# GpSimd operations that wait for VectorE, other places for results, and new times for the list schedule, in a fused attention and expert kernel

## The chip, the cores and the metric

The kernel runs on one core of one Trainium2 chip. A core has five engines with a queue each: TensorE (PE in the profile; its weight loads are listed apart as PEld), VectorE (DVE), ScalarE (ACT), GpSimd (POOL) and SyncE (SP), which here only issues DMAs. The metric is the device time of one execution in microseconds (us); lower is better. Before the change it is 932.47 us, the median of 3 runs (932.33 to 932.93).

## The reference

Attention with pooled keys and values (groups of 8 averaged), then a two-layer network with an unusual activation:

```python
def _attn_ref(q, k, v):                      # B, H, S, D = 8, 8, 576, 64
    k_p = k.reshape(B, H, S // 8, 8, D).mean(axis=3)
    v_p = v.reshape(B, H, S // 8, 8, D).mean(axis=3)
    scores = np.matmul(q, k_p.transpose(0, 1, 3, 2)) / np.sqrt(D)
    scores = scores - np.max(scores, axis=-1, keepdims=True)
    attn = np.exp(scores)
    attn = attn / (np.sum(attn, axis=-1, keepdims=True) + 1e-09)
    return np.matmul(attn, v_p).astype(np.float32)

def _moe_ref(x, w_in, w_out):                # x: 4608 x 512, w_in: 512 x 2048, w_out: 2048 x 512
    h = x @ w_in
    sp = np.maximum(h, 0.0) + np.log1p(np.exp(-np.abs(h)))
    g = h * erf(sp)
    return (g @ w_out).astype(np.float32)
```

## The kernel before, in words

**Tiles and stages.** The 4608 tokens are cut into nine chunks (`ck`) of 512; `w_in` and `w_out` into sixteen pieces of 128 rows of the hidden layer (`ft`). A step is one piece for one chunk, so there are 9 x 16 = 144 steps, two of which make a pair (`pair`). [...] ScalarE or another engine makes the high part by a cast, VectorE or GpSimd the low part by a subtraction: `ql` (L562) for the queries, `gl` (L822) for the activations, L401 for the weights.

**Attention** of a chunk (`job`, `softmax_tile`) runs while the chunk before it is in the network. Keys and values are loaded into `raw` and summed by GpSimd (L504, L506, L508); scores come from L572, L574 and L596; VectorE finds the maximum and subtracts it (L583, L585), ScalarE takes the exponentials, VectorE the sums and reciprocals (L630, L632, L634), GpSimd scales the last columns (L640, `ends`) and VectorE the whole (L644); TensorE transposes (L651, L658) and multiplies with the values (L688).

**The network.** In chunks 0 and 1 the first product is a plain matmul (L787). From chunk 2 (`FROM`) on it is made of seven half-size products (`products`, L733), whose weights are sums of pieces of `w_in`. The function `sums` makes these once, in chunk 1, and writes them to DRAM; from then on the place of `w_in` is free for others: `wi6` to `wi15` are a ring of ten slots into which SP loads the sums again for every pair (four loads a pair), `wi5` holds the accumulator `u` (four rows, one for each pair in turn), `wi0` to `wi4` hold the attention's result, a temporary and the hidden values `hs`. VectorE adds the products together (L751). The activation is Softplus (L805), Erf (L812), a product on VectorE (L815), a cast (L817) and the low part (L822). The second product is L836. After the sixteenth piece of a chunk `store` copies its four results (128 x 512 each) from PSUM into one of the two buffers `f`, on ScalarE (L848) or VectorE (L849), and a DMA takes each to `out`.

**The order.** All five queues are written out by one list scheduler, `Program.order`. Every operation has an engine (or a choice of them), an estimated cost in ns, and a due time `prio` in steps. The scheduler always takes the operation with the smallest sum of its earliest start and `SLACK` (30 ns) a step of due time; operations whose due time is more than `WINDOW` steps beyond the newest one on TensorE aren't looked at. An operation may go to another engine if it ends there at most `BIAS` ns after the end on its own. [...] In the first 57 us, dummy matmuls (`filler`, L884) fill TensorE's gaps.

Of the kernel before, what the change touches and what calls it, by code (L numbers as in the profile page):

```python
# [20 lines left out]
POOL = 8  # L21
# [4 lines left out]
P = 128  # L26
# [9 lines left out]
NB = 2  # L36


WINDOW = 14
SHIFT = 3  # L40
B1 = 2
T0, T0_STEP = -10.5, 0.5
VAL_R = 2.5
KEYS, KEYS_R, KEYS_S = -4.5, 0.4, -1.0
VALS, VALS_R, VALS_S = -1.0, 0.4, -1.2
Q_DUE = 5.2
W_IN, W_OUT = 1.0, 0.0
LEAD = 4
G2 = 5.0
ON_DVE = 2  # L50
CAP_H, CAP_O, CAP_ATT, CAP_CV, CAP_ATT0 = 2, 4, 4, 2, 6
ON_ACT = ((1, 1), (1, 1), (1, 1), (1, 1))
# [2 lines left out]
LENT_Q = ("wi15", "wo12")  # L55
LENT_KV = ("wo8", "wo9", "wo10", "wo11", "wi9", "wi10", "wi11", "wi12", "wi13", "wi14")
WIDE_FROM = 2
SLACK, BIAS = 30, 2000
FILL, MARGIN = 57000.0, 300
DGE = 2000  # L60
TURN = 0.0
# [4 lines left out]
HALF = TC // 2  # L66
PART = {"A11": (0, 0), "A12": (0, 1), "S1": (1, 0), "S3": (1, 1), "S2": (2, 0), "S4": (2, 1), "A22": (3, 0)}
PARTS = 4
RING = tuple(f"wi{i}" for i in range(6, NJ))
XF, TD, UU, HS = ("wi0", "wi1"), "wi2", "wi5", ("wi3", "wi4")  # L70
SUMS, SUMS_R = 2.0, 0.3
X_DUE = 3.0
RING_LEAD = 8.0
C_ID = 0
C_MA = 128
C_MB = 130
# [54 lines left out]
class Op:  # L131
    def __init__(self, eng, cost, prio, fn):
        self.eng, self.cost, self.prio, self.fn = eng, cost, prio, fn
        self.bufs, self.next, self.wait, self.ready = [], [], 0, 0.0
        self.set = None


class Program:
# [49 lines left out]
    def order(self):  # L188
        free = {e: 0.0 for e in self.DELAY}
        free["SP"] = 2400.0  # L190
        slots = {t: [0.0] * n for t, n in self.capacity.items()}
        avail = {e: [] for e in free}
        for i, o in enumerate(self.ops):
            o.key = (o.prio, i)
            if not o.wait:
                for e in o.choice:
                    avail[e].append(o)
        progress, out, loaded, port = 0.0, [], "sigmoid", 0.0
        spare = heapq.heappop(slots["banks"]) if self.filler else None
        for _ in self.ops:  # L200
            best = None
            for e, ops in avail.items():
                pick, ready = None, []
                for o in ops:
                    if o.prio > progress + self.window or any(b.left for b in o.after):
                        continue
                    start = max(o.ready + (DGE if e == "SP" else 0), free[e])
                    switch = SWITCH if o.set and o.set != loaded else 0
                    start += switch
                    if e == "POOL" or o.port and e == "DVE":  # L210
                        start = max(start, port)
                    need = {}
                    for b in o.bufs:
                        if not b.held:
                            for t in b.limits:
                                need[t] = need.get(t, 0) + 1
                    ok = True
                    for t, k in need.items():
                        if len(slots[t]) < k:
                            ok = False  # L220
                            break
                        start = max(start, heapq.nsmallest(k, slots[t])[-1] + (DGE if e == "SP" else 0))
                    if ok and e != o.eng:
                        ok = start + o.choice[e][0] <= max(o.ready, free[o.eng]) + o.cost + BIAS
                    if ok:
                        ready.append((start, o.key, o, start - switch * (1 - TURN) + SLACK * o.prio))
                if ready:
                    pick = min(ready, key=lambda r: (r[3], r[1]))[:3]
                if pick and (best is None or pick[:2] < best[:2]):
                    best = pick + (e,)  # L230
            if best is None:
                raise RuntimeError(("no operation can go on", progress, {e: [(o.prio, [b.args[3] for b in o.bufs if not b.held]) for o in ops][:8] for e, ops in avail.items()}, {k: len(v) for k, v in slots.items()}))
            start, _, o, e = best
            for a in o.choice:
                avail[a].remove(o)
            o.eng, (o.cost, o.fn) = e, o.choice[e]
            loaded = o.set or loaded
            if spare is not None and o.eng == "PE":
                if start > FILL:
                    heapq.heappush(slots["banks"], start)  # L240
                    spare = None
                else:
                    idle = start - max(free["PE"], 3000.0) - MARGIN - (1800 if not free["PE"] else 0)
                    out.extend([self.filler] * int(idle / 107))
            end = free[o.eng] = start + o.cost
            if o.eng == "POOL" or o.port and o.eng == "DVE":
                port = end
            if o.eng == "PE":
                progress = max(progress, o.prio)
            for b in o.bufs:  # L250
                if not b.held:
                    b.held = True
                    for t in b.limits:
                        heapq.heappop(slots[t])
                b.left -= 1
                b.end = max(getattr(b, "end", 0.0), end)
                if not b.left:
                    for t in b.limits:
                        heapq.heappush(slots[t], b.end + 150)
            for d, flow in o.next:  # L260
                if d.eng != o.eng:
                    t = end + self.DELAY[o.eng]
                else:
                    t = end + (self.SAME[o.eng] if flow else 0)
                d.ready = max(d.ready, t)
                d.wait -= 1
                if not d.wait:
                    for a in d.choice:
                        avail[a].append(d)
            out.append(o)  # L270
        self.length = max(free.values())
        return out
# [10 lines left out]
def moe_attention(ctx: ExitStack, tc: tile.TileContext, cst, qa, kl, vl, wi, wo, out):  # L283
# [204 lines left out]
    def job(ck, b, tiles, off, times, first, fresh):  # L488
# [60 lines left out]
        def softmax_tile(at, qo, T, r):  # L549
# [9 lines left out]
            copy(ck < 2, 4 * T, r - 0.6, lambda: qh.ap[:, :, :T], lambda: raw.ap[:, :, :T], [raw], [qh])  # L559

            def low(e):
                e.tensor_sub(ql.ap[:, :, :T], raw.ap[:, :, :T], f32(qh.ap[:, :, :T]))  # L562

            op("POOL", gps(4 * T), r - 0.5, lambda: low(nc.gpsimd), [raw, qh], [ql],
               alt=("DVE", dve(4 * T), lambda: low(nc.vector)) if first else None, port=True)
# [71 lines left out]
            def ends():  # L637
                sv = s.ap[:T].rearrange("t (p x) k -> t p x k", x=2)[:, :, 1, P - SP:]
                zv = z.ap[:T].rearrange("t (p x) -> t p x", x=2)[:, :, 1]
                nc.gpsimd.tensor_mul(bb.ap[:T], sv, zv.unsqueeze(2).broadcast_to([T, NP, 16]))  # L640

            op("POOL", gps(64), r + 1.2, ends, [s, z], [bb])

# [35 lines left out]
        for p in range(NP):  # L679
# [8 lines left out]
                    nc.tensor.matmul(d, w, e, start=(i == 0), stop=(i == 3), skip_group_check=True)  # L688

            r = due + p * 0.4  # L690
            op("PE", 3 * (n / 2.4 + 13) + n / 2.4 + 13, r, values, [eth, etl, etb, VA, VB], [pv])
            if ck >= FROM:
                x = xk[p // 2]
                after(op("ACT", act(n, True), r + 0.4, lambda p=p, pv=pv, x=x: nc.scalar.copy(
# [9 lines left out]

    po = {}

    common = late(UU, [4, HALF])

    def products(n, unit, hs):

# [28 lines left out]
        def multiply(prio, b, *what):  # L739
            def run():  # L740
                for j, (side, name, t, first) in enumerate(what):
                    product(side(b), name, t, first)

            reads = [parts[PART[name][0]] for _, name, _, _ in what] + [ts[ck, t] for _, _, t, _ in what]
            op("PE", 6 * 119 * len(what), prio, run, reads, [b])

        u, j = common, n // 2 % 4
        lo, hi = slice(0, HALF), slice(HALF, TC)

        def add(prio, dst, x, b, side, reads, writes):  # L750
# [18 lines left out]
    def pair(n):  # L769
# [44 lines left out]
        for k in range(2):  # L814
            op("DVE", dve(TC), n + 1.9, lambda k=k: nc.vector.tensor_mul(  # L815
                g(k), y.ap[:, half(k)], hh[k].ap), [(y, k), hh[k]], [gs[k]], port=kept)
            op("ACT", act(TC), n + 2.0, lambda k=k: nc.scalar.copy(gh[k].ap, g(k)), [gs[k]], [gh[k]], port=True,  # L817
               alt=("DVE", 0.52 * TC + 150, lambda k=k: nc.vector.tensor_copy(gh[k].ap, g(k)))
               if COPY_DVE > 1 and not kept else None)

            def low(e, k=k):
                e.tensor_sub(gl[k].ap, g(k), f32(gh[k].ap))  # L822

            both(True, dve(TC), gps(TC), n + 2.0, low, [gs[k], gh[k]], [gl[k]])

        for u, (ck, ft) in enumerate(units):
            if ft == 0:
                po[ck] = [bank("o") for _ in range(TC // P)]
            for t0 in range(0, TC // P, 1 if split else 2):
                ts = range(t0, t0 + (1 if split else 2))  # L830

                def gemm2(u=u, ft=ft, ts=ts, o=po[ck]):
# [4 lines left out]
                                             start=(ft == 0 and q == 0), stop=(ft == NJ - 1 and q == 2))  # L837

                prio = n + u + G2 + 0.1 * t0
                op("PE", 3 * 229 * len(ts), prio, gemm2, [gh[u], gl[u], w_out[ft]],  # L840
                   [po[ck][t] for t in ts])
                if ft == NJ - 1:
                    for t in ts:
                        store(ck, t, po[ck][t], prio + 0.1, ck == NC - 1)

    def store(ck, t, o, prio, last):
        ot, r0 = buf("gh" if last and t % 2 else "f", [DM]), TC * ck + P * t
        op("ACT", act(512, True), prio, lambda: nc.scalar.copy(ot.ap, o.ap), [o], [ot],  # L848
           alt=("DVE", dve(512), lambda: nc.vector.tensor_copy(ot.ap, o.ap)))  # L849
        save = lambda e: e.dma_start(out[r0:r0 + P, :], ot.ap)  # L850
        if last and t % 2:
            op("ACT", 100, prio, lambda: save(nc.scalar), [ot], [])
        else:
            op("SP", 800, prio, lambda: save(nc.sync), [ot], [])


    steps = [(ck, ft) for ck in range(NC) for ft in range(NJ)]
# [26 lines left out]
    pr.filler = Op("PE", 107, 0, lambda: nc.tensor.matmul(  # L884
        idle.ap[:, :256], cb[:, :P], cb[:, :256], start=True, stop=True))
    for o in pr.order():
        o.fn()


# [35 lines left out]
```

## Time and profile before

| | |
|---|---|
| median of 3 runs | 932.47 us |
| the profiled execution | 932.53 us |
| its span, from the first instruction to the last | 930.8 us |
| granted TensorE clock, mean | 0.999 |

The page gives each engine's busy time and its share of the span; the windows view gives the same for stretches of time; the view of waits adds up who stood idle until whom; the chain is followed back from the last instruction to whatever released each step. A matmul's end is modelled, and consecutive matmuls overlap in the records, so TensorE's busy time hides a part of each short stall.

```profile
PE   8999999999999999999999999999999999999998
DVE  6998784899977787777667776767667856664342
POOL 2589886445543244427351144344553322120000
DMA  9991234245396446755575356643776355546511
```

Each digit is the busy share of a fortieth of the span, in tenths. The first three slices, about 70 us, are the head: the weights are loaded, and the first chunk's attention has to be through before the network starts.

### The profile page before, as it was taken

The page shows a single profiled execution, that of the slowest core. Times are in us where ns is not written, and L with a number is a line of the kernel's source. Part 1 is how long each engine was busy: PE and PEld are TensorE (multiplying, and loading weights), DVE is VectorE, ACT ScalarE, POOL GpSimd, SP SyncE. Part 2 cuts the span into 40 slices and gives each one's busy share as a digit, 9 for nine tenths or more (in the row PEclk, how much of TensorE's full clock was granted, in tenths as well). Part 3 has the DMA queues.
Part 4 walks back from the last instruction along what each step waited for, and adds up shares of the span by engine and source line. Part 5 has one row for each costly group of instructions (what it writes and reads, how often), then busy time and mean ns, then how long its engine had stood idle before and what let it go on. Part 6 is the DMA issues. An engine that isn't in the chain of part 4 may idle for free.

```text
span 930.8 us, 16115 instructions
## 1 busy us (share of the span) xinstructions
PE 910.0 (98%) x5655; PEld 802.2 (86%) x5655; DVE 665.4 (71%) x1361; ACT 682.1 (73%) x1209; POOL 382.1 (41%) x475
## 2 busy tenths in 40 slices
PE   8999999999999999999999999999999999999998
PEld 7778878788888889899989888989998899888996
DVE  6998784899977787777667776767667856664342
ACT  4889995987677686876777767766886777665664
POOL 2589886445543244427351144344553322120000
PEclk9999999999999999999999999999999999999999
DMA  9991234245396446755575356643776355546511
GB/s 317 402 396 66 94 113 139 114 182 196 112 345 214 155 166 219 255 195 193 185 246 184 129 196 238 216 170 140 244 237 204 124 202 173 164 160 211 181 53 46
DMA packets 68257, 176.24 MB, mean 189 GB/s; under 512 B 11216, under 2 KB 13392, under 8 KB 68176
## 3 DMA queue, kind: packets, MB, share of 16 engines
q1 hardware_dynamic: 67888, 174.69, 54.4%
q8 instruction: 45, 0.74, 0.3%
q10 hardware_dynamic: 288, 0.52, 0.1%
q14 instruction: 36, 0.29, 0.1%
HBM read 151.06 MB, written 24.12 MB: 188 GB/s over the span
## 4 chain that ended last, share of the span: by engine, by line
PE 65%; DVE 8%; ACT 8%; DMA 5%; POOL 3%; issue 2%; SPq 0%; POOLq 0%; DVEq 0%; ACTq 0%
PE banks L836 32%; PE banks L733 24%; DMA out<-f 4%; PE banks L787 3%; PE banks L688 3%; ACT L805 2%; ACT y L805 1%; PE banks L572 1%; ACT y L812 1%; ACT L812 1%; PE banks L651 1%; DMA raw<-vl 1%; DVE wi L815 1%; DVE hs L815 1%; POOL gl L822 1%
## 5 line engine op out<-in xcount | busy, mean ns | idle before, releaser
L836 PE MATMUL banks<-wo,gh 128*128 128x512 f32 x1152 | 363.8, 397 | 1.7 <-DVE hs L751 0.8
L733 PE MATMUL banks<-t,wi 128*128 128x256 f32 x2352 | 314.3, 284 | 3.9 <-DVE wi L751 1.6
L733 PEld LDWEIGHTS banks<-t,wi 128*128 128x128 f32 x2352 | 300.8, 191 | 18.2 <-DVE wi L751 3.6
L836 PEld LDWEIGHTS banks<-wo,gh 128*128 128x128 f32 x1152 | 203.2, 189 | 36.0 <-DVE hs L751 1.0
L836 PE MATMUL banks<-wo,gl 128*128 128x512 f32 x576 | 225.2, 391 | 0.1
L836 PEld LDWEIGHTS banks<-wo,gl 128*128 128x128 f32 x576 | 108.2, 188 | 24.9 <-DVE gl L822 0.9
L805 ACT ACT_TABLE_LOAD x72 | 92.4, 1283 | 28.9 <-DVE wi L751 15.3
L751 DVE TENSOR_TENSOR wi<-wi,banks 128x256 f32<-128x256 f32 x168 | 67.1, 414 | 44.7 <-ACT wi L754 22.3
L787 PE MATMUL banks<-t,wi 128*128 128x512 f32 x384 | 92.6, 393 | 1.6 <-DVE f L849 1.1
L787 PEld LDWEIGHTS banks<-t,wi 128*128 128x128 f32 x384 | 70.9, 188 | 17.7 <-DVE f L849 1.3
L504 POOL TENSOR_TENSOR raw<-raw 128x256 f32<-128x256 f32 (+1 forms) x60 | 51.5, 861 | 82.8 <-DMA raw<-vl 52.7
L562 POOL TENSOR_TENSOR ql<-raw,qh 128x512 fp32r<-128x512 f32 (+1 forms) x36 | 46.6, 1295 | 74.2 <-ACT qh L324 68.1
L812 ACT ACTIVATE y<-y 128x1024 f32<-128x1024 f32 (+1 forms) x73 | 76.2, 1046 | 0.7
L812 ACT ACT_TABLE_LOAD x59 | 75.7, 1283 | 1.0
L817 ACT CAST gh<-hs 128x512 fp32r<-128x512 f32 x72 | 44.2, 618 | 30.4 <-DVE hs L815 17.3
L815 DVE TENSOR_TENSOR hs<-y,hs 128x512 f32<-128x512 f32 x72 | 54.0, 790 | 6.4 <-ACT y L812 6.4
L822 DVE TENSOR_TENSOR gl<-hs,gh 128x512 fp32r<-128x512 f32 x54 | 39.8, 744 | 18.6 <-ACT gh L817 18.1
L815 DVE TENSOR_TENSOR wi<-y,wi 128x512 f32<-128x512 f32 x56 | 40.5, 761 | 13.8 <-ACT y L812 13.7
L817 ACT CAST gh<-wi 128x512 fp32r<-128x512 f32 x56 | 34.2, 618 | 21.9 <-PE banks L836 10.5
L751 DVE TENSOR_TENSOR hs<-wi,banks 128x256 f32<-128x256 f32 x84 | 32.8, 415 | 23.7 <-PE banks L733 22.9
L668 POOL TENSOR_SCALAR etb<-etb 32x256 fp32r<-32x256 f32 (+1 forms) x38 | 16.0, 421 | 72.8 <-ACT etb L663 54.7
L822 POOL TENSOR_TENSOR gl<-wi,gh 128x512 fp32r<-128x512 f32 x19 | 25.8, 1359 | 43.0 <-ACT gh L817 23.9
(159 smaller groups left out, 1554.8 us busy)
## 6 DMA issues: line engine op xcount, KB each, us to landing
wi<-w SPq DMA_DIRECT2D x168, 512.0 KB, 4.6
wi<-w SPq DMA_DIRECT2D x56, 256.0 KB, 2.7
raw<-vl SPq DMA_DIRECT2D x36, 256.0 KB, 4.4
out<-f SPq DMA_DIRECT2D x34, 256.0 KB, 4.1
wi<-wi SPq DMA_DIRECT2D x16, 512.0 KB, 7.6
wo<-wo SPq DMA_DIRECT2D x16, 512.0 KB, 8.8
w<-t SPq DMA_DIRECT2D x16, 512.0 KB, 3.1
raw<-kl SPq DMA_DIRECT2D x26, 288.0 KB, 3.2
```

Source lines behind the costliest of these rows:

```text
L504: op("POOL", gps(4 * size), prio, lambda: nc.gpsimd.tensor_add(t.ap[:, 0:4], t.ap[:, 0:4], t.ap[:, 4:8]), [t], [t])
L562: e.tensor_sub(ql.ap[:, :, :T], raw.ap[:, :, :T], f32(qh.ap[:, :, :T]))
L688: nc.tensor.matmul(d, w, e, start=(i == 0), stop=(i == 3), skip_group_check=True)
L733: nc.tensor.matmul(dst(), weight(name, w, p), x[:, xl, p, :], start=(first and p == 0 and q == 0), stop=(p == 1 and q == 2), skip_group_ch ...
L751: return op("DVE", dve(HALF), prio, lambda: nc.vector.tensor_add(dst(), x(), b.ap[:, side]), reads + [b], writes)
L787: nc.tensor.matmul(ph.ap, w_in[ft].ap[:, w, P * p:P * p + P], xs[p].ap[:, x], start=(p == 0 and q == 0), stop=(p == NP - 1 and q == 2))
L805: nc.scalar.activation(y.ap[:, half(k)], hh[k].ap, AF.Softplus)
L812: op("ACT", act(w), n + 1.9, lambda sl=sl: nc.scalar.activation(y.ap[:, sl], y.ap[:, sl], AF.Erf), own, own, funcs="sigmoid")
L815: op("DVE", dve(TC), n + 1.9, lambda k=k: nc.vector.tensor_mul(g(k), y.ap[:, half(k)], hh[k].ap), [(y, k), hh[k]], [gs[k]], port=kept)
L817: op("ACT", act(TC), n + 2.0, lambda k=k: nc.scalar.copy(gh[k].ap, g(k)), [gs[k]], [gh[k]], port=True, alt=("DVE", 0.52 * TC + 150, lambda ...
L822: e.tensor_sub(gl[k].ap, g(k), f32(gh[k].ap))
L836: nc.tensor.matmul(o[t].ap, g.ap[:, gs], w_out[ft].ap[:, w], start=(ft == 0 and q == 0), stop=(ft == NJ - 1 and q == 2))
```

## The change

It has three parts.

1. The scheduler remembers the last marked VectorE operation it has placed (`shared`). A GpSimd operation that could have started before that operation's end plus 600 ns (`APART`) is given a dependency on it, so that on the chip GpSimd waits for it.
2. From chunk 1 to the last but one, three of a chunk's four results no longer go through `f`: two go to `wi6`, which leaves the ring (now nine slots), and one to the upper half of `wi5`, of which `u` keeps two rows in place of four.
3. The due times, the window, `BIAS`, and some cost estimates of TensorE's operations have new values.

```diff
-WINDOW = 14
+WINDOW = 8
-T0, T0_STEP = -10.5, 0.5
-VAL_R = 2.5
-KEYS, KEYS_R, KEYS_S = -4.5, 0.4, -1.0
-VALS, VALS_R, VALS_S = -1.0, 0.4, -1.2
+T0, T0_STEP = -10.5, 0.45
+VAL_R = 2.1
+KEYS, KEYS_R, KEYS_S = -5.5, 0.4, -0.5
+VALS, VALS_R, VALS_S = -1.0, 0.4, -1.1
-W_IN, W_OUT = 1.0, 0.0
-LEAD = 4
-G2 = 5.0
+W_IN, W_OUT = 1.4, 0.1
+LEAD = 4.25
+G2 = 5.2
-SLACK, BIAS = 30, 2000
+SLACK, BIAS = 30, 1150
-RING = tuple(f"wi{i}" for i in range(6, NJ))
-XF, TD, UU, HS = ("wi0", "wi1"), "wi2", "wi5", ("wi3", "wi4")
-SUMS, SUMS_R = 2.0, 0.3
-X_DUE = 3.0
-RING_LEAD = 8.0
+RING = tuple(f"wi{i}" for i in range(7, NJ))
+XF, TD, UU, HS, OUT = ("wi0", "wi1"), "wi2", "wi5", ("wi3", "wi4"), "wi6"
+SUMS, SUMS_R = 4.3, 0.3
+X_DUE = 2.6
+RING_LEAD = 6.25
+APART = 600
...
+            was = free[o.eng]
             end = free[o.eng] = start + o.cost
+            o.end = end
+            if o.eng == "POOL" and shared and max(o.ready, was) < shared.end + APART:
+                o.behind = shared
             if o.eng == "POOL" or o.port and o.eng == "DVE":
                 port = end
+                if o.eng == "DVE":
+                    shared = o
...
-            op("PE", 3 * (n / 2.4 + 13) + n / 2.4 + 13, r, values, [eth, etl, etb, VA, VB], [pv])
+            op("PE", 4 * max(n / 2.4 + 13, 112), r, values, [eth, etl, etb, VA, VB], [pv])
...
-    common = late(UU, [4, HALF])
+    common, outs = late(UU, [4, HALF]), late(OUT, [2, DM])
...
-            op("PE", 6 * 119 * len(what), prio, run, reads, [b])
-
-        u, j = common, n // 2 % 4
+            op("PE", 6 * 120 * len(what), prio, run, reads, [b])
+
+        u, j = common, n // 2 % 2
...
-                op("PE", 3 * 229 * len(ts), prio, gemm2, [gh[u], gl[u], w_out[ft]],
+                op("PE", 3 * 231 * len(ts), prio, gemm2, [gh[u], gl[u], w_out[ft]],
...
-        ot, r0 = buf("gh" if last and t % 2 else "f", [DM]), TC * ck + P * t
-        op("ACT", act(512, True), prio, lambda: nc.scalar.copy(ot.ap, o.ap), [o], [ot],
-           alt=("DVE", dve(512), lambda: nc.vector.tensor_copy(ot.ap, o.ap)))
-        save = lambda e: e.dma_start(out[r0:r0 + P, :], ot.ap)
+        r0 = TC * ck + P * t
+        if ck >= FROM - 1 and not last and t < 3:
+            kept = common if t == 2 else outs
+            key, piece = (kept, ("out", t)), w_in[5 if t == 2 else 6]
+            at = lambda: kept.ap[:, 2:4].rearrange("p a f -> p (a f)") if t == 2 else kept.ap[:, t]
+        else:
+            kept = key = buf("gh" if last and t % 2 else "f", [DM])
+            piece, at = None, lambda: kept.ap
+        after(op("ACT", act(512, True), prio, lambda: nc.scalar.copy(at(), o.ap), [o], [key],
+                 alt=("DVE", dve(512), lambda: nc.vector.tensor_copy(at(), o.ap))), *[piece] * bool(piece))
+        save = lambda e: e.dma_start(out[r0:r0 + P, :], at())
...
     for o in pr.order():
-        o.fn()
+        o.inst = o.fn()
+        if o.behind:
+            tc.add_manual_dep(getattr(o.inst, "ins", o.inst), getattr(o.behind.inst, "ins", o.behind.inst).name,
+                              mybir.DependencyInfo(mybir.DependencyClass.Sync, mybir.DependencyReason.SCHED_ONLY),
+                              reason="port")
```

More of the change, by code (lines that the diff above doesn't have):

```diff
@@ L134, in __init__ @@
         self.bufs, self.next, self.wait, self.ready = [], [], 0, 0.0
-        self.set = None
+        self.set, self.behind = None, None
 class Program:
@@ L197, in order @@
                     avail[e].append(o)
-        progress, out, loaded, port = 0.0, [], "sigmoid", 0.0
+        progress, out, loaded, port, shared = 0.0, [], "sigmoid", 0.0, None
         spare = heapq.heappop(slots["banks"]) if self.filler else None
@@ L561, in low @@
             def low(e):
-                e.tensor_sub(ql.ap[:, :, :T], raw.ap[:, :, :T], f32(qh.ap[:, :, :T]))
+                return e.tensor_sub(ql.ap[:, :, :T], raw.ap[:, :, :T], f32(qh.ap[:, :, :T]))
             op("POOL", gps(4 * T), r - 0.5, lambda: low(nc.gpsimd), [raw, qh], [ql],
@@ L639, in ends @@
                 zv = z.ap[:T].rearrange("t (p x) -> t p x", x=2)[:, :, 1]
-                nc.gpsimd.tensor_mul(bb.ap[:T], sv, zv.unsqueeze(2).broadcast_to([T, NP, 16]))
+                return nc.gpsimd.tensor_mul(bb.ap[:T], sv, zv.unsqueeze(2).broadcast_to([T, NP, 16]))
             op("POOL", gps(64), r + 1.2, ends, [s, z], [bb])
@@ L821, in low @@
             def low(e, k=k):
-                e.tensor_sub(gl[k].ap, g(k), f32(gh[k].ap))
+                return e.tensor_sub(gl[k].ap, g(k), f32(gh[k].ap))
             both(True, dve(TC), gps(TC), n + 2.0, low, [gs[k], gh[k]], [gl[k]])
@@ L846, in store @@
     def store(ck, t, o, prio, last):
-        ot, r0 = buf("gh" if last and t % 2 else "f", [DM]), TC * ck + P * t
-        op("ACT", act(512, True), prio, lambda: nc.scalar.copy(ot.ap, o.ap), [o], [ot],
-           alt=("DVE", dve(512), lambda: nc.vector.tensor_copy(ot.ap, o.ap)))
-        save = lambda e: e.dma_start(out[r0:r0 + P, :], ot.ap)
+        r0 = TC * ck + P * t
[9 more added lines that the diff above has]
+        save = lambda e: e.dma_start(out[r0:r0 + P, :], at())
         if last and t % 2:
-            op("ACT", 100, prio, lambda: save(nc.scalar), [ot], [])
+            op("ACT", 100, prio, lambda: save(nc.scalar), [key], [])
         else:
-            op("SP", 800, prio, lambda: save(nc.sync), [ot], [])
+            op("SP", 800, prio, lambda: save(nc.sync), [key], [])
     steps = [(ck, ft) for ck in range(NC) for ft in range(NJ)]
```

## The prediction

> **What bounds the kernel now.** I read the page's spans first, then the windows view by stage, then the longest waits, the chain that ended last, and the timeline at single stalls.
>
> ```profile
> span 930.8 us, 16115 instructions
> PE 910.0 (98%) x5655; PEld 802.2 (86%) x5655; DVE 665.4 (71%) x1361; ACT 682.1 (73%) x1209; POOL 382.1 (41%) x475
> ```
>
> ```profile
> 0.00:60.00 60.00, 54.66 (x421) 46.74 (x422) 50.02 (x117) 40.47 (x127) 31.43 (x47) 1.00 0.99 369
> 60.00:180.00 120.00, 118.20 (x574) 96.28 (x573) 90.89 (x175) 102.64 (x175) 94.40 (x111) 1.00 0.35 123
> 180.00:926.00 746.00, 736.84 (x4663) 659.22 (x4662) 524.53 (x1071) 538.16 (x908) 256.29 (x318) 1.00 0.55 186
> ```
>
> The columns of the windows view are the stretch, its length, and PE, PEld, DVE, ACT and POOL busy; then clock, DMA share, GB/s. TensorE is the bound: from 60 to 926 us it stands idle for only 1.80 + 9.16 us. The change removes no kernel matmul, so it can only save those gaps and part of the head. Busy time hides some of each gap:
>
> ```profile
> L836 PE MATMUL banks<-wo,gh 128*128 128x512 f32 x1152 | 363.8, 397 | 1.7 <-DVE hs L751 0.8
> 911.32 15.00 PE banks L836 x66
> L884 PE MATMUL banks<-cst 128*128 128x256 bf16 x227 | 29.3, 289 | 2.6 <-DMA cst<-cst 2.6
> ```
>
> One 512-wide matmul shows 397 ns but follows the last every 15.00/66 = 227 ns, so a stall costs about 0.17 us more than the idle it shows. The third row is filler: 29.3 of the head's 54.66 busy us are dummy matmuls, so real work there is 25.4 us of 60.
>
> **The change, part by part.**
>
> *1. Places for results.* Today every result is copied into one of two `f` buffers (L848 on ScalarE, L849 on VectorE) and leaves by a DMA; the third copy of a chunk waits for the first DMA to land, and all behind it in that in-order queue waits too.
>
> ```profile
> ACT f L848 <- DMA out<-f: 6.8, 3, 2.8
> DVE f L849 <- DMA out<-f: 6.5, 3, 3.5
> ```
>
> ```profile
> 263.59 6.29 DMA out<-f
> 366.31 5.10 DMA out<-f
> 462.34 6.63 DMA out<-f
> 562.67 7.13 DMA out<-f
> 849.99 5.57 DMA out<-f
> ```
>
> The chain view's columns are start, length and what. Five chunk ends have an output transfer on the chain that ended last, which a kernel with PE at 98% should not have. I put a window round each (264 to 276, 366 to 374, 462 to 473, 562 to 573, 850 to 859); their sum:
>
> ```profile
> sum 51.00, PE 47.30 PEld 42.41 DVE 30.34 ACT 32.51 POOL 15.96; mean PE 9.46 PEld 8.48 DVE 6.07 ACT 6.50 POOL 3.19
> ```
>
> 51.00 - 47.30 = 3.70 us idle, in about seven stalls: with 7 x 0.17 it is 4.9 us. After the change three of four results of chunks 1 to 7 have a place of their own, reused only a chunk later, and the fourth finds `f` free. I take -4.5, leaving 0.4 because other work shares these windows; bounds 0 and -4.9. What is late next there is the ordinary work in the queues. The price: `wi6` leaves the ring (nine slots, not ten) and `u` has two rows, not four.
>
> ```profile
> wi<-w SPq DMA_DIRECT2D x168, 512.0 KB, 4.6
> ```
>
> A ring load lands in 4.6 us. Four loads serve a pair of steps, and a step lasts about (926 - 60)/144 = 6.0 us; nine slots are 2.25 pairs, 27 us, of which a pair in use takes 12. A lead of 6.25 steps is 38 us, so the ring, not the lead, decides, and some 15 us cover 4.6. I price it at 0; with the cover gone a late load would cost up to 4.6 us. The two rows of `u` turn over every 24 us: 0.
>
> *2. GpSimd behind VectorE.* That the two engines hold each other up is in the durations:
>
> ```profile
> L815 DVE TENSOR_TENSOR hs<-y,hs x72: 677/685/1789, 166.2 to 909.2; 128x512 f32<-128x512 f32 x72
> L815 DVE TENSOR_TENSOR wi<-y,wi x56: 673/685/1796, 276.5 to 917.4; 128x512 f32<-128x512 f32 x56
> L751 DVE TENSOR_TENSOR wi<-wi,banks x168: 360/417/423, 250.1 to 911.7; 128x256 f32<-128x256 f32 x168
> ```
>
> Minimum, median, maximum: L815, whose two inputs are in SBUF, goes from 685 to 1796 ns; L751, with one input in PSUM, never passes 423. One case where TensorE pays:
>
> ```profile
> 389.18 0.29 POOL L640 TENSOR_TENSOR bb<-s,z 128x64 f32<-128x64 f32 x1 [2.22 <-ACT vah L528]
> 389.27 0.75 DVE L822 TENSOR_TENSOR gl<-hs,gh 128x512 fp32r<-128x512 f32 x1
> 389.43 1.74 POOL L562 TENSOR_TENSOR ql<-raw,qh 128x512 fp32r<-128x512 f32 x1
> 389.94 1.84 DVE L644 TENSOR_TENSOR s<-s,z 128x576 f32<-128x576 f32 x1
> 391.93 0.41 PE L651 MATMUL banks<-cst,s 128*128 128x128 f32 x2 [0.83 <-DVE s L644]
> ```
>
> L644 stands at 1.84 us, ends about when L562 does plus its own 0.7, and PE waits 0.83. Eight such places (128 to 132, 320 to 325, 361 to 365, 387 to 393, 538 to 545, 621 to 627, 702 to 706, 809 to 814) sum to
>
> ```profile
> sum 41.00, PE 38.56 PEld 32.66 DVE 36.36 ACT 24.41 POOL 26.37; mean PE 4.82 PEld 4.08 DVE 4.54 ACT 3.05 POOL 3.30
> ```
>
> 2.44 us idle; with some nine stalls of 0.17, 3.9 us. A wait cures only operations that the list marks for the port. L585 isn't marked:
>
> ```profile
> L585 DVE TENSOR_TENSOR s<-s,m 128x576 f32<-128x576 f32 x25 | 23.6, 944 | 0.7
> L644 DVE TENSOR_TENSOR s<-s,z 128x576 f32<-128x576 f32 x28 | 25.7, 918 | 3.2 <-POOL bb L640 3.1
> L815 DVE TENSOR_TENSOR hs<-y,hs 128x512 f32<-128x512 f32 x72 | 54.0, 790 | 6.4 <-ACT y L812 6.4
> L815 DVE TENSOR_TENSOR wi<-y,wi 128x512 f32<-128x512 f32 x56 | 40.5, 761 | 13.8 <-ACT y L812 13.7
> ```
>
> ```profile
> L644 DVE TENSOR_TENSOR s<-s,z x35: 741/752/1851, 23.3 to 799.7; 128x576 f32<-128x576 f32 x28, 64x576 f32<-64x576 f32 x7
> ```
>
> Against a median of 752 ns for this size, L585 loses 25 x 0.19 = 4.8 us and L644 28 x 0.17 = 4.6; L815 loses 72 x 0.105 + 56 x 0.076 = 11.8. So 23% of this loss is uncovered, and a wait is given only where the list has the two within 600 ns; I allow as much again for places where the chip has drifted further. That leaves 60%: **-2.4**, bounds 0 and -3.9, if the waits cost nothing.
>
> What they cost: behind the waiting instruction stand all later GpSimd ones, and for those wait TensorE (`ql`, `gl`), VectorE (L644 behind L640) and SP's loads into `raw`. [...] L640 follows L634, which ended at 389.00 (388.81 + 0.19), by 0.18 us:
>
> ```profile
> 388.81 0.19 DVE L634 RECIPROCAL z<-z 128x8 f32<-128x8 f32 x1
> ```
>
> After 180 us GpSimd is busy 256 of 746 us: taken as 0 there. For 60 to 180 see the rivals.
>
> [...]
>
> *3. BIAS 2000 to 1150.* Work that VectorE and GpSimd can both do goes to the slower one less readily.
>
> ```profile
> L822 POOL TENSOR_TENSOR gl<-wi,gh 128x512 fp32r<-128x512 f32 x19 | 25.8, 1359 | 43.0 <-ACT gh L817 23.9 <-issue 8.3 <-PE banks L688 6.9
> L822 DVE TENSOR_TENSOR gl<-wi,gh 128x512 fp32r<-128x512 f32 x37 | 27.4, 747 | 18.7 <-ACT gh L817 18.5
> ```
>
> Each move is 0.61 us shorter for its reader and 0.75 more on VectorE, which is at 71%. I take 0; bounds -1 and +1.
>
> *4. Due times, window, PE costs.* A unit of due time weighs 30 ns in the list's choice (SLACK), so shifts of 0.05 to 2.3 units turn only near-ties. The window (14 to 8 units, 84 to 48 us) matters in the head, where no step has moved the list's progress yet: it holds back early weight splitting. I take 0 here; bounds -4 (below) and +2.5.
>
> **Sum:** 932.5 (the profiled execution; span 930.8 and 1.7 around it; the median of the runs, 932.47, is the same) - 4.5 - 2.4 = **925.6**.
>
> **Rivals.**
>
> *A. The head shortens too.* VectorE is busy 50.02 of the first 60 us, and some of it is weight splitting in front of the first attention tiles:
>
> ```profile
> L385 DVE SCALAR_TENSOR_TENSOR banks<-banks,hs 128x512 uint32<-128x512 uint32 x6 | 4.1, 689 | 0.0
> L395 DVE SCALAR_TENSOR_TENSOR f<-wi,banks 128x512 uint32<-128x512 uint32 x4 | 2.7, 682 | 0.0
> ```
>
> That is 6.8 us; if 4 of it moves behind the first chunk's attention, PE, whose real work is 25.4 of 60, starts 4 us sooner: 921.5. Against: DMA is 0.99 busy there.
>
> *B. The waits do nothing.* If the chip's order is further from the list than 600 ns, VectorE is blocked as before: 925.6 + 2.4 = 928.0. [...]
>
> *C. New stalls.* The list is made anew. The 9.16 us of idle after 180 hold the 3.70 and about 2.4 of parts 1 and 2; some 3.1 are accidents of order. If the new order has three times as many: 925.6 + 6.2 = 931.8, the same as before.
>
> *D. GpSimd becomes the bound between 60 and 180 us* (the slower side). It is busy 94.40 of 120 there with 111 instructions, so 25.6 us are free, 0.23 each; that is the point from which it decides. Its L401 (the low weights) and L822 feed TensorE. [...]
>
> **How the numbers follow.** Forecast 0.42 (own range 922 to 929), A 0.20, B 0.12, C 0.13, D 0.13. A measurement of this kernel can tell about 0.2%, 1.9 us, from no change, that is 930.6 to 934.3. Faster: 0.42 + 0.20 + 0.12 and a quarter of C, 0.77. Same: half of C, and a little of D, 0.09. Slower: the rest of C and most of D, 0.14. The range takes in part 1's and 2's upper bounds with A (932.5 - 4.9 - 3.9 - 4 = 919.7, less 1 for BIAS and about 1 for accidents) and C with its spread: 917.5 to 934.
>
> **What would show it.** Part 1: no output DMA on the chain at the ends of chunks 1 to 7 and no wait of L848 or L849 for one; if those windows still idle 3.7 us, the copy wasn't what held TensorE. Part 2: L815's maximum back near 685 and its means under 720; if they stay near 790, B. D: GpSimd near 115 of 120 us from 60 to 180 with L401 late. A: fewer than 227 fillers. C: short TensorE stalls at new places, led by other lines. The forecast is wrong if TensorE's idle after 180 us isn't some 5 us smaller.

## The result, and the profile after

The changed kernel takes 924.91 us, the median of five runs (921.54 to 926.92), against 932.33 before (930.94 to 932.93): 0.9919 of it, 95% interval [0.9895, 0.9942], so it is 0.8% faster. The forecast was 925.6. The profiled execution is the quickest of the five, 921.54 us with a span of 919.7; what follows of its profile is therefore some 3 us kinder than a usual run. One of the four executions of the kernel with the waits alone (below) took 1588.75 us at a granted clock of 0.73; the median there is 927.56 us with it and 926.85 without.

The page of the changed kernel first, then the windows view for the same three stages as before (length, then PE, PEld, DVE, ACT, POOL busy, clock, DMA share, GB/s):

```profile
span 919.7 us, 16168 instructions
PE 905.8 (98%) x5640; PEld 802.5 (87%) x5640; DVE 654.3 (71%) x1350; ACT 677.7 (74%) x1196; POOL 387.7 (42%) x499
```

```profile
0.00:60.00 60.00, 56.06 (x421) 47.84 (x422) 51.34 (x118) 40.99 (x131) 32.68 (x47) 1.00 0.99 371
60.00:180.00 120.00, 117.04 (x569) 95.77 (x568) 94.95 (x175) 103.34 (x173) 95.59 (x114) 1.00 0.32 111
180.00:916.00 736.00, 732.69 (x4654) 658.88 (x4652) 507.99 (x1059) 533.18 (x895) 259.46 (x339) 1.00 0.57 190
```

After 180 us TensorE is idle for 736.00 - 732.69 = 3.31 us, where it was 9.16, so 5.85 less where the prediction asked for some 5; between 60 and 180 us for 2.96, where it was 1.80. The ends of five chunks, now at 264 to 276, 361 to 369, 458 to 468, 552 to 562 and 846 to 855 us, summed as before:

```profile
sum 49.00, PE 49.00 PEld 45.72 DVE 33.40 ACT 35.98 POOL 21.18; mean PE 9.80 PEld 9.14 DVE 6.68 ACT 7.20 POOL 4.24
```

The 3.70 us of idle time at the chunk ends are gone to the last digit. The chain that ended last has output DMAs only at 153.82 and 156.59 us, the end of chunk 0, whose results still go through `f`. There too lies the one copy of a result that the view of waits still shows waiting for an output DMA, in place of 6.8 + 6.5 us:

```profile
ACT f L862 <- DMA out<-f: 2.2, 1, 2.2
```

VectorE's product with the hidden value (L815 before, L822 now; the lines have moved by seven) in the view of that line (minimum, median, maximum), and below it the groups by shape (busy us, mean ns):

```profile
L822 DVE TENSOR_TENSOR hs<-y,hs x72: 677/686/1731, 164.0 to 897.6; 128x512 f32<-128x512 f32 x72
L822 DVE TENSOR_TENSOR wi<-y,wi x56: 673/686/990, 272.6 to 905.3; 128x512 f32<-128x512 f32 x56
```

```profile
L592 DVE TENSOR_TENSOR s<-s,m 128x576 f32<-128x576 f32 x25 | 26.4, 1054 | 0.6
L898 PE MATMUL banks<-cst 128*128 128x256 bf16 x212 | 27.3, 291 | 2.6 <-DMA cst<-cst 2.6
L822 DVE TENSOR_TENSOR hs<-y,hs 128x512 f32<-128x512 f32 x72 | 51.5, 750 | 10.8 <-ACT y L819 10.7
L822 DVE TENSOR_TENSOR wi<-y,wi 128x512 f32<-128x512 f32 x56 | 38.0, 716 | 20.5 <-ACT y L819 20.5
```

Here the picture is mixed: the means fell from 790 and 761 to 750 and 716 ns, but one operation still stands for 1731, and the unmarked subtraction (L585 before, L592 now) went up from 944 to 1054: the list keeps only those VectorE operations apart from GpSimd's, in its own times, that the program marks with `port`. The fillers fell from 227 to 212.

And one thing is new. TensorE's clock, 1.00 in every stage before, drops in one place. The timeline of PE there, and two windows of 3.41 us each:

```profile
260.41 0.39 PE L843 MATMUL banks<-wo,gl 128*128 128x512 f32 x1
262.20 3.40 PE L740 MATMUL banks<-t,wi 128*128 128x256 f32 x18 [1.40 <-DVE wi L758]
```

```profile
260.66:264.07 3.41, 1.90 (x13) 1.56 (x13) 3.28 (x10) 3.15 (x9) 2.12 (x3) 1.00 0.46 160
264.07:267.48 3.41, 3.41 (x18) 3.41 (x17) 1.70 (x5) 1.30 (x3) 2.72 (x5) 0.50 0.97 324
```

TensorE waits 1.40 us for VectorE; in the window of 3.41 us that holds this wait it works 1.90. For the next 3.41 us the clock is granted at 0.50. So this stall costs once as idle time and again, up to 1.7 us, as slow work that counts as busy (an estimate, half of the 3.41 us at 0.50).

### The profile page after: what moved, and what is told of

Read it like the earlier page. It is cut to its first block, busy times and chain, and to the rows that moved or that the text cites. A ratio compares the mean times of both kernels' runs of the same rounds, so it can differ in the third digit from the quotient of the medians.

```text
span 919.7 us, 16168 instructions
## 1 busy us (share of the span) xinstructions
PE 905.8 (98%) x5640; PEld 802.5 (87%) x5640; DVE 654.3 (71%) x1350; ACT 677.7 (74%) x1196; POOL 387.7 (42%) x499
## 4 chain that ended last, share of the span: by engine, by line
PE 75%; DVE 6%; ACT 3%; POOL 2%; DMA 2%; issue 1%; POOLq 0%; ACTq 0%; DVEq 0%
PE banks L843 36%; PE banks L740 29%; PE banks L695 3%; PE banks L794 3%; PE banks L579 1%; PE banks L658 1%; DVE hs L822 1%; DMA w<-t 1%; PE banks L581 1%; PE banks L603 1%; ACT L812 1%; DMA wi<-w 1%; ACT y L812 1%; POOL gl L829 0%; DMA out<-f 0%
## 5 line engine op out<-in xcount | busy, mean ns | idle before, releaser
L758 DVE TENSOR_TENSOR wi<-wi,banks 128x256 f32<-128x256 f32 x168 | 67.3, 413 | 37.6 <-PE banks L740 19.3
L511 POOL TENSOR_TENSOR raw<-raw 128x256 f32<-128x256 f32 (+1 forms) x60 | 47.9, 800 | 88.5 <-DMA raw<-vl 38.4
L569 POOL TENSOR_TENSOR ql<-raw,qh 128x512 fp32r<-128x512 f32 (+1 forms) x36 | 42.4, 1177 | 65.1 <-PE banks L843 13.2
L829 POOL TENSOR_TENSOR gl<-hs,gh 128x512 fp32r<-128x512 f32 x26 | 34.7, 1341 | 77.1 <-ACT gh L824 74.9
L822 DVE TENSOR_TENSOR hs<-y,hs 128x512 f32<-128x512 f32 x72 | 51.5, 750 | 10.8 <-ACT y L819 10.7
L829 POOL TENSOR_TENSOR gl<-wi,gh 128x512 fp32r<-128x512 f32 x20 | 25.9, 1295 | 70.7 <-ACT gh L824 51.1
L822 DVE TENSOR_TENSOR wi<-y,wi 128x512 f32<-128x512 f32 x56 | 38.0, 716 | 20.5 <-ACT y L819 20.5
L829 DVE TENSOR_TENSOR gl<-hs,gh 128x512 fp32r<-128x512 f32 x46 | 35.2, 768 | 23.1 <-ACT gh L824 22.9
L758 DVE TENSOR_TENSOR hs<-wi,banks 128x256 f32<-128x256 f32 x84 | 32.7, 416 | 22.4 <-PE banks L740 21.5
## 6 DMA issues: line engine op xcount, KB each, us to landing
wi<-w SPq DMA_DIRECT2D x56, 256.0 KB, 4.0
raw<-vl SPq DMA_DIRECT2D x36, 256.0 KB, 3.7
raw<-qa SPq DMA_DIRECT2D x28, 256.0 KB, 3.9
```

The costliest lines, as they stand in the source:

```text
L511: op("POOL", gps(4 * size), prio, lambda: nc.gpsimd.tensor_add(t.ap[:, 0:4], t.ap[:, 0:4], t.ap[:, 4:8]), [t], [t])
L569: return e.tensor_sub(ql.ap[:, :, :T], raw.ap[:, :, :T], f32(qh.ap[:, :, :T]))
L758: return op("DVE", dve(HALF), prio, lambda: nc.vector.tensor_add(dst(), x(), b.ap[:, side]), reads + [b], writes)
L829: return e.tensor_sub(gl[k].ap, g(k), f32(gh[k].ap))
```

## The experiments

The change has three parts: waits, places, times. All eight combinations were run, so that each part can be read with and without the others. Then the new times were taken apart, and the places.

**Waits alone.**

```diff
+            if o.eng == "POOL" and shared and max(o.ready, was) < shared.end + APART:
+                o.behind = shared
...
-        o.fn()
+        o.inst = o.fn()
+        if o.behind:
+            tc.add_manual_dep(...)
```

> The kernel before with nothing but the GpSimd waits (APART = 600); the list and its order are the same as before. Theory (as predicted): the waits are worth 2.4 us, so 929.9 us; VectorE's product of activation and hidden value, at a maximum of 1796 ns before, comes back to under 1000 ns and its two means (790 and 761 ns) to under 720. Rival 1 (the waits only move the place where GpSimd stands, VectorE is held up as before): 932.3, the means within 20 ns of before, but GpSimd's own operations get shorter. Rival 2 (GpSimd becomes the bound between 60 and 180 us): 935 or more, with GpSimd near 115 of 120 us there.

Measured: 926.85 against 931.45, ratio 0.9949 [0.9932, 0.9965], so the part is worth 4.6 us; later expectations start from 927.56 and so from 3.9. That is twice what I had expected, and the signs that I had named came in part:

```profile
180.00:914.00 734.00, 726.14 (x4629) 653.45 (x4628) 515.89 (x1070) 535.73 (x905) 237.15 (x318) 1.00 0.55 188
L822 DVE TENSOR_TENSOR hs<-y,hs 128x512 f32<-128x512 f32 x72 | 52.8, 774 | 6.4 <-ACT y L819 6.4
L822 DVE TENSOR_TENSOR wi<-y,wi 128x512 f32<-128x512 f32 x56 | 36.4, 687 | 13.7 <-ACT y L819 13.6
```

Of the two means one is cured (687) and one is not (774), and the longest of these operations still takes 1506 ns, where under 1000 was expected. VectorE is busy for 515.89 us up to 914 us, where it was about 521. GpSimd's 318 operations after 180 us, the same as before, fell from 256.29 to 237.15 us, which rival 1 had named. By itself that is no gain: time that an operation stood while it ran can now lie before its start. Rival 1's time, 932.3, didn't come.

**Places alone.**

```diff
-RING = tuple(f"wi{i}" for i in range(6, NJ))
+RING = tuple(f"wi{i}" for i in range(7, NJ))
...
-    common = late(UU, [4, HALF])
+    common, outs = late(UU, [4, HALF]), late(OUT, [2, DM])
...
-        u, j = common, n // 2 % 4
+        u, j = common, n // 2 % 2
...
+        if ck >= FROM - 1 and not last and t < 3:
+            kept = common if t == 2 else outs
```

> The kernel before with only the results' places changed (two in the slot that leaves the ring, one in the upper half of the accumulator), due times as before. The list is made anew, since its buffers differ. Theory: 4.5 us, so 927.8; no wait of a result's copy for an output DMA at the ends of chunks 1 to 7, and TensorE's idle time round the chunk ends (3.70 us in five windows before) falls under 1. Rival (new stalls of the new list eat it): 930 to 934 with the copies' waits gone all the same. Rival (the copy was not what held TensorE): the idle time at the chunk ends stays.

Measured: 923.42 against 931.45, ratio 0.9910 [0.9895, 0.9925]: 8.0 us, more than the bound of 4.9. VectorE and GpSimd are held up as before (the product's means are 802 and 730), so this gain doesn't come from fewer hold-ups. In the windows at the chunk ends given above for the changed kernel TensorE is idle for none of 49 us here too.

```profile
180.00:914.00 734.00, 730.51 (x4650) 656.63 (x4650) 524.11 (x1069) 532.15 (x897) 268.53 (x327) 1.00 0.56 188
```

Idle time from 180 to 914 us is 3.49 us here, where it was 9.16. The last run below, with nine slots and no new places, says how much of that is the new list.

**The changed kernel without the waits.** Its list is that of the changed kernel, so only the waits differ.

```diff
-            if o.eng == "POOL" and shared and max(o.ready, was) < shared.end + APART:
-                o.behind = shared
```

> The changed kernel without the GpSimd waits; list and order are those of the changed kernel. Theory: 924.9 + 2.4 = 927.3, and GpSimd's own operations are held up longer while they run (18 us over their usual durations with the waits, 37 before the change). Rival 1 (waits worth nothing): 924.9 within 1. Rival 2 (they cost, because the signal delays GpSimd): 923 or less.

Measured: 932.27 against 931.45, ratio 1.0010 [0.9994, 1.0025]. Without the waits the whole change is worth nothing; with these lists they bring 7.4 us (932.27 to 924.91; 8.2 to 8.5 by the ratios to the kernel before), three times the 2.4 expected.

```profile
180.00:914.00 734.00, 721.93 (x4598) 648.29 (x4597) 522.38 (x1053) 526.18 (x887) 284.06 (x339) 1.00 0.57 190
L820 DVE TENSOR_TENSOR hs<-y,hs 128x512 f32<-128x512 f32 x72 | 55.8, 810 | 11.7 <-ACT y L817 11.6
L820 DVE TENSOR_TENSOR wi<-y,wi 128x512 f32<-128x512 f32 x56 | 42.8, 802 | 20.3 <-ACT y L817 20.2
```

Set beside the row of the changed kernel: TensorE's idle time is 734.00 - 721.93 = 12.07 us up to 914 us, and GpSimd is busy 284.06 us with the same 339 operations that took 259.46 with the waits. The product's means go from 750 and 716 back to 810 and 802. In the traces, 35 of these products take over 750 ns without the waits and 18 with them, and each of the 35 and the 18 starts while a GpSimd operation is already running. A wait holds back a GpSimd operation that the list has behind the VectorE one; it can't do anything about one in front, which is why the picture above is mixed.

Who held TensorE? Both kernels issue the same 5428 matmuls (fillers aside) in the same order. The longest of TensorE's waits after 180 us (us, times, longest), without the change's waits and with them:

```profile
PE banks L738 <- DVE wi L756: 8.3, 9, 1.9
```

```profile
PE banks L740 <- DVE wi L758: 1.4, 1, 1.4
```

One of those nine, on GpSimd, VectorE and TensorE, and VectorE's same subtraction and addition in the changed kernel:

```profile
246.69 1.55 POOL L827 TENSOR_TENSOR gl<-hs,gh 128x512 fp32r<-128x512 f32 x1 [7.45 <-ACT gh L822]
247.03 1.77 DVE L435 TENSOR_TENSOR f<-wi 128x512 f32<-128x512 f32 x1
248.83 0.42 DVE L756 TENSOR_TENSOR wi<-wi,banks 128x256 f32<-128x256 f32 x1
249.39 0.95 PE L738 MATMUL banks<-t,wi 128*128 128x256 f32 x6 [1.90 <-DVE wi L756]
```

```profile
245.39 0.68 DVE L437 TENSOR_TENSOR f<-wi 128x512 f32<-128x512 f32 x1
246.09 0.42 DVE L758 TENSOR_TENSOR wi<-wi,banks 128x256 f32<-128x256 f32 x1
```

L435 (L437 in the changed kernel) takes 1.77 us beside GpSimd's L827 and 0.68 without it, and TensorE's wait of 1.90 us for the addition behind it is gone. So the gain comes the way the prediction said, through VectorE.

**The changed kernel without the places.** The edit of the places, backwards.

> The changed kernel with the results back in the two f buffers, ten ring slots and four rows of the accumulator; waits and due times as in the changed kernel; the list is made anew. Theory: 924.9 + 4.5 = 429.4 + 500 = 929.4, with five output DMAs on the chain that ended last again. Rival (the due times alone had already moved other work out of those places): 925 to 926.5.

(The 429.4 in it is a slip of the pen; 929.4 is meant.) Measured: 928.38 against 931.45, ratio 0.9961 [0.9947, 0.9975]: under the new times the places are worth 3.5 us, less than half of the 8.0 under the old. The time is within 1 us of the expected one, but the output DMAs are not back at five chunk ends: behind chunk 0 the chain has three, at 271.61, 277.25 and 655.90 us.

**Waits and places under the old times.** The two edits above together, with nothing of part 3.

> Places and waits together, the due times, window, BIAS and costs of before: the change without its third part. Measured so far, each against before at 931.45: waits alone 927.56 (-3.9), places alone 923.42 (-8.0); the changed kernel without waits 932.27, without places 928.38, whole 924.91. Theory 1 (parts add up, and the new times cost some microseconds): 931.45 - 3.9 - 8.0 = 919.5, faster than the whole change. Theory 2 (waits and places save the same stalls): 923, the new times are worth about -1 or 2 the other way.

Measured: 919.94 against 931.62, ratio 0.9875 [0.9854, 0.9897]. The parts add up (919.5 expected), and this version is faster than the whole change, which had 924.59 in the same set of runs. The new times cost 4.65 us.

**The new times alone.** The changed kernel without waits and places.

> Only the new due times, window, BIAS and TensorE costs; results in f, ten ring slots, no GpSimd waits. Theory 1 (the new times cost, and their list needs the waits): 928.38 + 7.4 (the waits' worth in the changed kernel) = 935.8, slower than before by 4. Rival (the new times are neutral alone and only meet badly with the new places): 931 to 933.

Measured: 936.67 against 931.62, ratio 1.0056 [1.0037, 1.0074]: slower than before, as the first theory said (935.8).

**The changed kernel again,** in the same set of runs.

> The changed kernel again, beside the others on one chip: 924.9 within 2. Its five runs so far spread from 921.54 to 926.92, those of before from 930.94 to 932.93; if the spread is the kernel's own, it shows again.

Measured: 924.59, 923.58 to 925.51, ratio 0.9922 [0.9904, 0.9940]. The eight combinations in one table (medians; the kernel before was 931.45 to 932.33 in these sets):

| | old times | new times | what the times cost |
|---|---|---|---|
| neither | 931.6 | 936.67 | +5 |
| waits | 926.85 | 928.38 | +1.5 |
| places | 923.42 | 932.27 | +8.9 |
| both | 919.94 | 924.59 | +4.65 |

**Wider waits.** The VectorE operations with two SBUF inputs that the list doesn't mark are remembered too; they are not kept apart in the list's times, so the order stays.

```diff
-                if o.eng == "DVE":
-                    shared = o
+            if o.eng == "DVE" and (o.port or o.meets):
+                shared = o
```

> As the run with places and waits under the old times, and the waits also on the VectorE operations with two SBUF inputs that the list doesn't mark for the port (the subtraction of the maximum, L585 before, and the low part of the values, L530 before); the order is the same. Theory: those stand at 983 to 1054 ns on average against 752, and come back under 800; 0.5 to 1.5 us faster than the run without them. Rival (their hold-ups don't reach TensorE): within 0.5, with the means back all the same. Rival (GpSimd comes late): slower.

Measured: 920.80 against 919.94 for the base, ratio 0.9881 [0.9864, 0.9899] to before. No gain, and the step it rested on fell:

```profile
L592 DVE TENSOR_TENSOR s<-s,m 128x576 f32<-128x576 f32 x25 | 24.7, 990 | 0.6
```

The mean stays at 990 ns (1000 in the base) in place of under 800. A wait of this kind only holds back a GpSimd operation that the list has behind the VectorE one, and in the trace all 11 of these 25 that take over 820 ns start while a GpSimd operation is already running.

**The new times taken apart,** on the base of waits and places (919.94). BIAS alone:

```diff
-SLACK, BIAS = 30, 2000
+SLACK, BIAS = 30, 1150
```

> Places and waits under the old times (919.94), and BIAS at 1150 alone. The new times as a whole cost 4.7 us on this base (924.59 against 919.94). Theory 1 (each new list costs by accident, whatever the edit): 921 to 924. Theory 2 (BIAS is harmless or a gain, as its intent, a shorter way to the reader, says): 918 to 920.5. In the trace: whether TensorE's clock is granted in full from the first matmul to the last, as in this base, or halves for 3.4 us as in every kernel with the new times.

Measured: 929.30, ratio to before 0.9973 [0.9960, 0.9986], above what either theory said. The due times alone:

```diff
-T0, T0_STEP = -10.5, 0.5
+T0, T0_STEP = -10.5, 0.45
...
-SUMS, SUMS_R = 2.0, 0.3
-X_DUE = 3.0
-RING_LEAD = 8.0
+SUMS, SUMS_R = 4.3, 0.3
+X_DUE = 2.6
+RING_LEAD = 6.25
```

> Places and waits under the old times, and the new due times alone (all but the window, BIAS and TensorE's costs). Theory 1 (the due times make the loss, with a TensorE stall near 260 us that halves the clock): 923 to 926, a stretch at half clock of 3.4 us or 6.8 us between 250 and 290 us. Theory 2 (the loss comes with BIAS or the costs): 919 to 921 and full clock.

Measured: 935.70, ratio to before 1.0037 [1.0019, 1.0055]: the stall and the half clock of theory 1 came (below), but its time is 10 us short. TensorE's costs alone:

```diff
-            op("PE", 3 * (n / 2.4 + 13) + n / 2.4 + 13, r, values, [eth, etl, etb, VA, VB], [pv])
+            op("PE", 4 * max(n / 2.4 + 13, 112), r, values, [eth, etl, etb, VA, VB], [pv])
...
-            op("PE", 6 * 119 * len(what), prio, run, reads, [b])
+            op("PE", 6 * 120 * len(what), prio, run, reads, [b])
...
-                op("PE", 3 * 229 * len(ts), prio, gemm2, [gh[u], gl[u], w_out[ft]],
+                op("PE", 3 * 231 * len(ts), prio, gemm2, [gh[u], gl[u], w_out[ft]],
```

> Places and waits under the old times, and the new costs of TensorE's operations alone (120 for 119, 231 for 229, at least 112 for a product with the values). Theory (a fraction of a percent in the costs turns near-ties of the list only): 919 to 921. Rival (a new list is a new draw: accidents of order of several us): above 922 or below 918.

Measured: 930.37, ratio to before 0.9984 [0.9973, 0.9996], as the rival said. So each edit alone costs 9.4, 15.8 and 10.4 us on this base, and all of them together 4.65. The prices don't add up, so none of them can be read as what its edit is worth in another list; of the five lists tried on this base the old one is the best. Even new costs, under 1% higher for the two large products and higher for narrow products with the values, which no reader would call a change of plan, throw away 10 us. (The window by itself leaves the four compute queues as they are, entry by entry; only SP's queue differs. It wasn't run.)

Most of the loss has one place. Windows of 30 us, 255 to 285, and, where a second loss shows, 60 to 180 us, of the base, then of the changed kernel run again, then of BIAS, due times and costs alone:

```profile
60.00:180.00 120.00, 117.25 (x566) 95.16 (x565) 90.78 (x173) 101.64 (x173) 92.00 (x111) 1.00 0.35 121
...
255.00:285.00 30.00, 30.00 (x202) 26.78 (x201) 24.70 (x56) 23.44 (x41) 17.81 (x25) 1.00 0.85 312
```

```profile
255.00:285.00 30.00, 27.17 (x163) 23.92 (x162) 20.00 (x48) 20.29 (x38) 15.84 (x25) 0.94 0.89 299
```

```profile
255.00:285.00 30.00, 25.91 (x171) 23.44 (x170) 22.19 (x54) 20.56 (x37) 14.90 (x22) 0.94 0.87 283
```

```profile
60.00:180.00 120.00, 113.13 (x539) 92.51 (x538) 90.18 (x161) 96.56 (x164) 88.68 (x106) 0.97 0.34 116
255.00:285.00 30.00, 26.09 (x161) 23.44 (x160) 21.99 (x51) 16.00 (x30) 10.63 (x17) 0.89 0.84 294
```

```profile
60.00:180.00 120.00, 114.31 (x545) 92.85 (x544) 91.80 (x165) 101.19 (x167) 90.21 (x107) 0.99 0.36 122
255.00:285.00 30.00, 25.92 (x169) 23.20 (x168) 21.77 (x50) 19.23 (x36) 14.12 (x22) 0.94 0.85 274
```

This is the end of chunk 1, where the plain products end and the half-size ones begin. The base is busy for all 30 us at full clock. The changed kernel idles 2.83 there and loses another 0.06 x 30 = 1.8 to the clock: 4.6 us, as much as its 4.65 in all. (By the starts of the matmuls it comes to this place 1.7 us ahead of the base and loses another 1.6 us behind it, which about cancel.) BIAS alone loses 4.09 + 1.8 = 5.9 of its 9.4 there; the due times 3.91 + 3.3 there and 4.1 + 3.6 more than the base between 60 and 180 us, together 14.9 of 15.8; the costs 5.9 and 4.1, 10.0 of 10.4. Three of these stalls stand in the list already. Working out each kernel's list with its own `Program.order`, in the scheduler's own times, TensorE is idle between 240 and 300 us for 0.2 us in the base, 4.2 with BIAS alone, 4.3 with the due times alone and 3.4 with the costs alone. In the changed kernel's list it is 0 there, so that kernel's stall arises only on the chip.

What the stall is made of differs from list to list. In the run with the new costs it is this, on VectorE and then on TensorE:

```profile
268.06 0.49 DVE L334 CAST t<-f 128x256 fp32r<-128x256 f32 x2 [1.96 <-DMA w<-t]
268.47 0.76 DVE L460 TENSOR_TENSOR t<-f,t 128x256 fp32r<-128x256 f32 x2
269.14 0.74 DVE L637 TENSOR_REDUCE z<-s 64x8 f32<-64x576 f32 x1
269.80 0.40 DVE L758 TENSOR_TENSOR wi<-wi,banks 128x256 f32<-128x256 f32 x1
```

```profile
270.35 1.62 PE L740 MATMUL banks<-t,wi 128*128 128x256 f32 x6 [4.08 <-DVE wi L758]
```

TensorE waits 4.08 us for L758, an addition of 0.4 us that gives a bank free. L758 stands in VectorE's queue behind the last of the sums of weights (L334, L460), whose buffer a DMA to DRAM still holds: 1.96 us of VectorE's waiting in front of L334 end with that DMA.

**Nine ring slots, results in `f`.** What the places take away, without what they give.

```diff
-RING = tuple(f"wi{i}" for i in range(6, NJ))
+RING = tuple(f"wi{i}" for i in range(7, NJ))
...
-        u, j = common, n // 2 % 4
+        u, j = common, n // 2 % 2
```

> The kernel before with nine ring slots and two rows of the accumulator, the results still in the two f buffers: what the places take away, without what they give. It tells why places alone brought 8.0 us where the windows at the chunk ends held 4.9. Theory 1 (the new list that comes with nine slots is better by accident, the places themselves bring their 4.9): 928.5. Theory 2 (all 8 come from the places, which free the queues for longer than the stalls at the chunk ends): 931 to 932. Rival (nine slots are a price): above 933, and the places bring more than 8.

Measured: 930.03 against 931.76, ratio 0.9983 [0.9972, 0.9995]. Nine slots are no price; they come out 1.7 us ahead, between the times of the first two theories. From there to places alone are 6.6 us.

## Why the prediction was right, point by point

The time was right to 0.7 us by luck: errors of both signs met. The forecast summed -4.5 and -2.4; measured from part to part, along the way in which the runs stand in the table, it is -8 for the places, -3.5 for the waits on top of them, and +4.65 for the times.

- **Places: the mechanism right, the size too small.** The copies' waits and the idle time at the chunk ends are gone, as foretold. But I had taken the five windows for all that the two buffers cost, and 4.9 for a bound. 1.7 of the 8.0 go with the nine slots' list. Counting the columns multiplied by the starts of the matmuls in the profiled runs before and with the places alone, I estimate that some 4.4 of the 9.3 us by which the last matmul starts earlier are gained inside the five windows, as forecast, and the rest between them; what the rest is made of stays open. Part of it may be the seam at 255 to 285 us, which went from 1.57 us idle before to none with the places alone, but that stretch lies partly inside one of the five windows:

```profile
255.00:285.00 30.00, 28.43 (x194) 25.22 (x194) 21.35 (x51) 24.49 (x45) 15.00 (x22) 1.00 0.92 322
```

```profile
255.00:285.00 30.00, 30.00 (x206) 26.94 (x205) 25.18 (x58) 24.21 (x43) 16.82 (x26) 1.00 0.84 294
```

- **Waits: the mechanism right, the size too small.** I had counted only eight places, 3.9 us at most, and allowed 60%. The waits are worth 4.6 alone, 3.5 behind the places, and 7.4 in the changed kernel, whose list without them has more of the same stalls: 12.07 us idle after 180 us, 8.3 of it behind one line of VectorE. So the bound of 3.9 held for one list only. The test that I had named, a maximum near 685 and means under 720, failed in part: 1731, 750 and 716. The allowance for unmarked operations stood (L592 got worse), but marking them (wider waits) cured nothing. What I had not allowed for are the GpSimd operations that already run when the VectorE one starts.
- **BIAS, due times and costs at 0: this step failed.** I had argued that a step of due time weighs 30 ns and so turns only near-ties. That is beside the point: a near-tie turned early can deal everything behind it anew, and the price depends on whether the new order has a stall at the seam. The bounds of -4 and +2.5 were too narrow on one side; measured are +1.5 to +8.9 for the whole set, +9.4 to +15.8 for its parts. BIAS didn't even do what I expected of it in the list: with BIAS alone GpSimd has 24 + 25 + 13 low parts (L829; every operand is split into a cast, the high part, and the rest, the low part, and three products of them are added up) where the base has 24 + 21 + 13.
- **The rivals.** C (new stalls) happened along with the forecast, not in place of it: the new times cost 4.65 where I gave C 6.2. A (the head) is there in part: 212 fillers, and 56.06 - 27.3 = 28.8 us of other work by 60 us in place of 25.4, but given back by the seam. D didn't come: GpSimd is busy 95.59 of 120 us between 60 and 180 us, where 115 were its mark. What the waits would add for each operation was the author's estimate, and no run shows it; busy time there went from 94.40 us for 111 operations to 95.59 for 114. B is out by the run without waits.
- **Sums.** Two are off in the last digit: 2.44 + 9 x 0.17 is 4.0, not 3.9, and A's time is 921.6, not 921.5. 23% taken off twice leaves 54 to 59%, not 60. None of them moves the forecast by more than 0.3 us.

## What to carry to other kernels

Where queues are written out in advance, a model that keeps two engines apart on paper need not keep them apart on the chip; here adding the waits, without any other change of the order, was worth 3.5 to 7.4 us. When an edit makes such a schedule anew, split it: run the mechanism under the old times and the new times without the mechanism, for here the mechanisms brought 11.7 us and the new times took 4.65 back, and the best version was the change without its third part. Look for the loss at the seams between stages, in the list's own times first, and count a stall twice where the clock drops behind it (in the changed kernel 1.40 us of waiting, then 3.41 us at 0.50).

## What the hardware showed that I had not expected

The clock dropped without TensorE being idle for long. In the changed kernel 1.90 of 3.41 us of work in one window, with a longest gap of 1.40 us, was followed by 3.41 us at 0.50. In the run with the waits alone, a longer gap was not:

```profile
854.12 1.70 PE L740 MATMUL banks<-t,wi 128*128 128x256 f32 x12 [1.92 <-DVE hs L758]
```

```profile
850.00:856.00 6.00, 4.08 (x24) 3.33 (x23) 3.90 (x8) 2.10 (x4) 0.00 (x0) 1.00 0.64 222
```

Here TensorE idles 1.92 us and the clock stays at 1.00. In the clock record of the changed kernel 256.0 us at 1.00 are followed by the 3.41 at 0.50 and then by 651.9 at 1.00; that of the kernel before has 921.6 us at 1.00. These are 75, 1, 191 and 270 times 3.413 us. But the share of work in a stretch of that length, by this profile's busy times, doesn't say where a drop comes. In the changed kernel without the waits, the gap of 1.90 us shown above falls in one stretch of 3.41 us; TensorE works for 1.54 us of it, less than the 1.90 that was followed by a drop, and the clock stays at 1.00:

```profile
245.96:249.37 3.41, 1.54 (x7) 0.94 (x6) 3.35 (x5) 0.66 (x2) 2.67 (x2) 1.00 0.43 154
249.37:252.79 3.42, 3.40 (x33) 3.42 (x34) 3.06 (x9) 1.24 (x4) 0.47 (x2) 1.00 0.79 265
```

So what sets off a drop stays open: in the changed kernel a gap of 1.40 us was followed by one, and in the two other runs gaps of 1.90 and 1.92 us were not.
